# A causal mask added by VectorE, value sums in column quarters, and set-up loads on ScalarE's queue, in a two-layer memory transformer

## The chip, the cores and the metric

The kernel runs on one core of one Trainium2 chip. A core has TensorE (PE: matmuls, with its weight loads shown as PEld), VectorE (DVE), ScalarE (ACT), GpSimd (POOL) and SyncE (SP), which work side by side and are held together by semaphores; 16 DMA engines move data. Matmuls write into PSUM, eight banks of 128 partitions by 512 float32; everything else lives in SBUF. The metric is the device time of one execution in microseconds; the kernel before has a median of 1535.17 us over five runs (1532.09 to 1537.07).

## The reference

Two rounds of the same two layers, A and B, on x of 2048 rows by 448 columns, all in bfloat16:

```python
x = x + _A_ref(_layernorm(x), A_mem0, A_Wq, A_Wk, A_Wv, A_Wo, A_seg_len)
x = x + _B_ref(_layernorm(x), B_W_gate, B_W_up, B_W_down)
x = x + _A_ref(_layernorm(x), A_mem0, A_Wq, A_Wk, A_Wv, A_Wo, A_seg_len)
x = x + _B_ref(_layernorm(x), B_W_gate, B_W_up, B_W_down)
```

A is an attention with a memory that is carried from segment to segment (16 heads of 256, memory M = 8 rows, segments of 32 rows, 64 segments):

```python
mask = (idx[:, None] < M) | (idx[:, None] >= idx[None, :])
mem = mem0
for s in range(n_seg):
    h = concatenate([mem, x[:, s*32:(s+1)*32, :]])           # 40 rows
    q, k, v = h @ Wq, h @ Wk, h @ Wv                         # per head
    p = softmax(where(mask, q @ k.T * scale, -1e9))
    o = (p @ v) @ Wo                                         # summed over heads
    mem = o[:, :M, :]
    outs.append(o[:, M:, :])
```

B is a gated feed-forward layer, `(relu(h @ W_gate) * (h @ W_up)) @ W_down`, with 1792 hidden columns. The rows of one segment depend on those before it only through `mem`, eight rows, so the 64 segments of a round form a chain.

## The kernel before, in words

**What is precomputed.** In set-up, the products M = Wq Wk^T (for the scores) and N = Wv Wo (for the values) are made per head (`products`). Wq, Wk and Wv come in by transposing DMAs of 1024 columns each (`wT`), Wo by plain DMAs (`wo`), each into one of eight slots of the tile `big`. Later the same memory holds U (value sums of both layers), UR (the rider's sums, below) and the feed-forward weights Wg, Wu, Wgu3 and Wd, so those loads wait until the slots are done with.

**The steps.** 68 steps t run one segment of the first round (layer 0) beside one of the second round (layer 1), which lags by four segments. Partitions or columns 0 to 63 mostly hold layer 0, 64 to 127 layer 1. One step, in `step`:

- `h_nat`: the segment's 40 rows per layer, hT, transposed by a DMA into hK.
- `t_units`: hT times M, in five units of row-tiled matmuls (tH) and two full ones (tF) each; copies to TTm (memory queries) and TTs (segment queries) by ACT or DVE (tEm, tEs).
- `s_mem`, the memory rows' scores and softmax (smem, smx), `p_t_mem` (ptm: transposed by TensorE into PTm), `u_mem` (umem: hK times PTm, copied to UTm), `un_mem` (unm: UTm times N, 112 matmuls in four column quarters). ACT copies half the result (XH, L1007), DVE adds the rest (X, L1010, two operations), and `m_t` (mt: five matmuls with the 0/1 matrix selm) puts the new memory into the next step's hT (mtE). This is the chain from step to step.
- `s_seg`, the segment rows' scores (sseg) and softmax (ssx, L860 to L870): maximum, subtraction, exponential (ACT), sum, reciprocal, product into Ps. A DMA transposes Ps into PTs. `u_seg` (useg0 to 3) multiplies hK by PTs, and copies (usE) go to U or UR.
- In every second step: `un`, U times N, for two segments; the layer norm `ln_b`; the feed-forward layer `glu` (glH row-tiled, glF full) and its down product (dn); `out`.

**Riders.** For odd pairs of segments 3 to 29, layer 1's value sums are not made by a matmul of their own: 16 rows of them at a time are copied from UR into free columns of UTm (`ride`, on POOL) and go through unm along with the memory. In those pairs `un` has only layer 0's 64 rows (unc), and so has every pair at the start and end; unc and its down product dnc (first and last pairs only) run as two column halves of the array.

**The causal mask** is a bf16 tile maskr with 0 or -1.6e10. In sseg, the first matmul multiplies it by the identity, which starts the accumulation in PSUM, and the scores are added to it by the matmuls that follow.

**The order.** The program doesn't run its operations as they are written. `_Order` collects them with estimated costs, and a list scheduler fixes the order on each engine at build time, from estimated start times, priorities (BIAS by kind of operation, PERIOD, MODEPEN for a change of tiling mode), SLACK, and RESERVE (PSUM banks kept free). A matmul group has a mode: FULL, ROWS (two 64-row tiles), COLS2, COLS4; a change is charged with SWITCH. `_Sched` then adds semaphore waits. On each engine instructions are issued in the fixed order; one that waits holds all behind it. All DMAs are issued by SP, in one queue.

**Lines.** All matmuls have line L134. L642 and L643 are the copies by ACT and by DVE or POOL; L704 wT, L707 wo, L760 to L766 the feed-forward loads, L806 the transpose of xnA, L926 that of Ps, L940 that of hT; L865, L866, L867, L868, L869 and L870 the softmax; L799 the normalisation in both layer norms.

Of the kernel before, what the change touches and what calls it, by code (L numbers as in the profile page):

```python
# [9 lines left out]
ALU = mybir.AluOpType  # L10
AX = mybir.AxisListType

D = 448
# [153 lines left out]
class _Op:  # L167
    __slots__ = ("i", "kind", "eng", "cost", "fn", "rd", "wr", "name", "mode", "preds", "succs", "prio", "np", "fin", "alloc", "tiles", "ready",
                 "fixed", "bq", "start", "base")


class _Order:
# [11 lines left out]
    def add(self, kind, eng, cost, fn, rd, wr, name=None, mode=0, base=None):  # L184
        o = _Op()
        o.i = len(self.ops)
        o.kind, o.eng, o.cost, o.fn, o.rd, o.wr, o.name, o.mode = kind, eng, cost, fn, list(rd), list(wr), name, mode
        o.succs, o.np, o.alloc, o.ready, o.fixed, o.base = [], 0, [], None, None, base
        self.ops.append(o)
        return o  # L190
# [41 lines left out]
    def ready_at(self, o, e):  # L232
        by = {}
        for q in o.preds:
            if q.fixed == e == "pe":
                continue
            k = q.name if q.fixed == "sp" else q.fixed
            if by.get(k, 0.0) < q.fin:
                by[k] = q.fin
# [8 lines left out]
    def run(self):  # L248
# [40 lines left out]
        while len(order) < total:  # L289
            best = None  # L290
            for e in self.ENGS:
# [7 lines left out]
                if e == "pe":  # L299
                    lst = [(t, o, t + (self.SWITCH if o.mode != mode else 0.0)) for t, o in lst]  # L300
# [4 lines left out]
                for t, o, x in lst:  # L305
                    if x <= lim:
                        p = o.prio
                        if e == "pe" and o.mode != mode:
# [21 lines left out]
            if e == "pe" and o.mode != mode:  # L330
                dur += self.SWITCH
                occ += self.SWITCH
                mode = o.mode
# [24 lines left out]
    def emit(self):  # L358
# [3 lines left out]
        for o in self.order:  # L362
            if o.fixed == "pe":
                self.sc.pe(o.fn(), res(o.rd), res(o.wr), o.fin)
            elif o.fixed == "sp":
                self.sc.dma(o.name, o.fn, res(o.rd), res(o.wr), o.fin)
# [4 lines left out]
BIAS = {"dn.1": -104633.0, "dn.3": -214049.0, "dn.9": -140910.0, "dnE": -786.0, "dnc.11": -139309.0, "dnc.3": 13831.0, "dnc.5": -27812.0,  # L371
    "dnc.7": -6924.0, "glE": -27693.0, "glF0.1": 10010.0, "glF0.11": -174653.0, "glF0.3": -145944.0, "glF0.5": -92812.0, "glF0.7":
    -177072.0, "glF0.9": 19897.0, "glF1.1": -143065.0, "glF1.11": -138570.0, "glF1.3": -105265.0, "glF1.5": -5540.0, "glF1.7": -174301.0,
    "glF1.9": -29011.0, "glF2.1": -153282.0, "glF2.11": -52540.0, "glF2.3": -138423.0, "glF2.5": -124385.0, "glF2.7": -1692.0, "glF2.9":
    -137772.0, "glF3.1": 5447.0, "glF3.3": -104010.0, "glF3.5": 54496.0, "glF3.7": -100124.0, "glF3.9": -120145.0, "glH0.1": 9143.0,
    "glH0.11": -23267.0, "glH0.5": 8524.0, "glH0.7": -139206.0, "glH0.9": 50271.0, "glH1.1": 546.0, "glH1.11": 6320.0, "glH1.3": -616.0,
    "glH1.5": 2773.0, "glH1.7": -2514.0, "glH1.9": 6624.0, "glH2.1": -2112.0, "glH2.11": 2748.0, "glH2.3": -130475.0, "glH2.5": 7362.0,
    "glH2.7": -149344.0, "glH2.9": -112454.0, "glH3.1": -48434.0, "glH3.11": -22235.0, "glH3.3": -113185.0, "glH3.5": 2935.0, "glH3.7":
    3071.0, "glH3.9": -98605.0, "hk": -31963.0, "init": 10044.0, "lna": -13048.0, "lnaC": -8463.0, "lnaT": 25587.0, "lnb": -18913.0, "lnbT":
    -8397.0, "lnbT.11": -8604.0, "lnbTE": 11209.0, "mem": 67030.0, "mt": 400.0, "mt.0": 831.0, "mt.1": -109166.0, "mt.10": -250.0, "mt.2":  # L380
    -28509.0, "mt.3": 7483.0, "mt.5": -625.0, "mt.6": -4647.0, "mt.7": -202.0, "mt.8": -21362.0, "mt.9": -48020.0, "mtE": 11874.0, "prodE":
    11527.0, "prodM.4": 1944.0, "prodN.4": 60.0, "ptm.0": -28767.0, "ptm.1": -55591.0, "ptm.10": -24031.0, "ptm.2": -28108.0, "ptm.3":
    508.0, "ptm.4": 3242.0, "ptm.5": 727.0, "ptm.6": -3533.0, "ptm.7": 929.0, "ptm.8": -1615.0, "ptm.9": -180.0, "ptmE": 1366.0, "pts":
    -38980.0, "pts.11": -20130.0, "ptsE": 1167.0, "ride": 2087.0, "rt": 511.0, "rtT": 13707.0, "smem.0": 20701.0, "smem.1": -2955.0,
    "smem.10": 20594.0, "smem.2": 4096.0, "smem.3": -4245.0, "smem.4": 3195.0, "smem.5": 2453.0, "smem.6": 1626.0, "smem.7": -130185.0,
    "smem.8": -140597.0, "smem.9": 2798.0, "smx": 36317.0, "sseg.1": -387.0, "sseg.10": -79467.0, "sseg.11": 11143.0, "sseg.2": 952.0,
    "sseg.3": 6076.0, "sseg.4": -71071.0, "sseg.5": 282.0, "sseg.6": 279.0, "sseg.7": -132491.0, "sseg.8": -52625.0, "sseg.9": 8111.0,
    "ssx": 5698.0, "tEm": -1049.0, "tEs": -133776.0, "tF0.0": 2987.0, "tF0.1": -445.0, "tF0.10": 4587.0, "tF0.11": 5600.0, "tF0.2": -4684.0,
    "tF0.3": -118385.0, "tF0.4": -349.0, "tF0.5": 3028.0, "tF0.6": -8779.0, "tF0.8": 5120.0, "tF0.9": 51.0, "tF1.1": 5328.0, "tF1.10":
    -11710.0, "tF1.11": -88005.0, "tF1.2": -29557.0, "tF1.3": -6535.0, "tF1.4": 143.0, "tF1.5": 881.0, "tF1.7": -121537.0, "tF1.8":  # L390
    -120291.0, "tF1.9": 850.0, "tF2.0": -27387.0, "tF2.1": -2633.0, "tF2.10": 9137.0, "tF2.11": -433.0, "tF2.2": 14432.0, "tF2.3": -876.0,
# [857 lines left out]
```

## Time and profile before

| | |
|---|---|
| median of five runs | 1535.17 us |
| the profiled execution, in all | 1536.47 us |
| its span, first to last instruction | 1534.7 us |
| mean granted clock of TensorE | 0.994 |
| mask matmuls: 60 of 256 columns, 8 of 128 | 16.4 us busy for the 60, ends modelled |
| unc matmuls, 64 weight columns x 448 | 1008, mean 354 ns |
| unm matmuls, 32 weight columns x 224 | 7504, mean 262 ns |
| rider copies on POOL | 56, mean 961 ns |
| Wo loads, 896 KB, issue to landing | 4, median 6.1 us |
| Wq, Wk and Wv transposes, issue to landing | 4 each, medians 5.9, 5.9, 8.2 us |
| gate and up loads of 448 KB, down loads of 784 KB, to landing | medians 4.6, 6.9 and 7.6 us |

The span is cut into windows, into groups of like instructions, and into a chain of waits that is followed back from the end. Matmuls are pipelined: several are in flight at once, their ends are modelled, and a mean duration is longer than the distance between two starts. So costs of matmuls are read from start to start in the timeline. The idle time before an instruction carries the name of the event that ended it. The granted clock is 1.00 nearly everywhere, 0.50 from about 84 to 97 us and from about 166 to 169 us.

### The profile page before, as it was taken

Reading aid. Unit: us, or ns where it says so; the run is one execution under the profiler, and the core shown is the slowest. Engines: PE = TensorE matmul, PEld = TensorE weight load, DVE = VectorE, ACT = ScalarE, POOL = GpSimd, SP = SyncE. Lnnn points to the kernel's source line nnn. Section 1 sums busy time; section 2 is a strip of 40 time slices with the busy share of each in tenths; the row PEclk is TensorE's granted clock in tenths of the full one; section 3 lists DMA queues with packets and bytes.
Section 4 is the critical chain, followed back from the end, with each engine's and each line's share of the span. In section 5 each row is a group of like instructions: output and inputs, shape, how many; then the busy total and the mean of one; then the engine's idle time right before and its main releaser. Section 6 shows DMA issues by size and latency. Waiting matters only on the chain.

```text
span 1534.7 us, 72243 instructions
## 1 busy us (share of the span) xinstructions
PE 1471.2 (96%) x33360; PEld 1157.7 (75%) x33360; DVE 720.9 (47%) x1911; ACT 797.6 (52%) x2363; POOL 92.4 (6%) x142
## 2 busy tenths in 40 slices
PE   4989998999999999999999999999999999999998
PEld 2568777787878777887877778787877788787776
DVE  4425354543545455344545454354545534453444
ACT  5734555554555546555555555555554555545453
POOL 1000000000000000000000000000000000000000
PEclk9989999999999999999999999999999999999999
DMA  9941111121111111111111111111111111111110
GB/s 216 222 113 33 23 30 24 25 27 25 33 25 29 25 32 28 20 29 29 28 24 34 24 25 27 25 33 24 30 24 33 25 23 30 28 27 25 27 28 18
DMA packets 186462, 59.50 MB, mean 39 GB/s; under 512 B 175256, under 2 KB 185264, under 8 KB 186160
## 3 DMA queue, kind: packets, MB, share of 16 engines
q1 hardware_dynamic: 186160, 54.88, 18.4%
q8 instruction: 262, 4.29, 1.1%
q14 instruction: 40, 0.33, 0.1%
HBM read 10.33 MB, written 1.84 MB: 8 GB/s over the span
## 4 chain that ended last, share of the span: by engine, by line
PE 83%; DVE 6%; DMA 5%; ACT 2%; SPq 2%; issue 1%; POOL 0%
PE P L134 83%; DMA PTs<-Ps 2%; DMA xBT<-xnB 2%; SPq L704 2%; DVE big L643 1%; ACT big L642 1%; DVE xnA L799 1%; DVE X L1010 1%; DVE stat L868 1%; DMA big<-in_A_Wq_dram 1%; DVE stat L865 0%; ACT XH L1007 0%; DMA big<-in_A_Wo_dram 0%; DVE XA L1170 0%; DVE stat L792 0%
## 5 line engine op out<-in xcount | busy, mean ns | idle before, releaser
L134 PE MATMUL P<-hT,Mw 128*128 128x80 bf16 (+1 forms) x11424 | 421.9, 200 | 0.3 <-ACT Mw L642 0.2
L134 PEld LDWEIGHTS P<-hT,Mw 128*128 128x128 bf16 x11424 | 403.0, 100 | 9.2 <-ACT Mw L642 0.3
L134 PE MATMUL P<-Nw,big 128*64 128x448 bf16 (+1 forms) x1904 | 283.9, 353 | 1.4
L642 ACT ACTIVATE TTm<-P 128x96 bf16<-128x96 f32 (+2 forms) x593 | 143.7, 242 | 248.5 <-PE P L134 242.4
L642 ACT ACTIVATE TTs<-P 128x384 bf16<-128x384 f32 (+2 forms) x582 | 263.2, 453 | 0.4 <-DVE TTm L643 0.2
L134 PEld LDWEIGHTS P<-Nw,big 128*64 128x64 bf16 (+1 forms) x1904 | 136.2, 104 | 108.7 <-issue 3.1
L134 PE MATMUL P<-xBT,big 128*128 128x128 bf16 (+3 forms) x3808 | 212.3, 216 | 2.8 <-DMA xBT<-xnB 2.8
L134 PEld LDWEIGHTS P<-xBT,big 128*128 128x128 bf16 (+1 forms) x3808 | 181.0, 97 | 25.0 <-issue 11.1
L134 PE MATMUL P<-Nw,UTm 128*32 128x224 bf16 x7504 | 195.9, 262 | 2.8 <-ACT UTm L642 2.8
L134 PEld LDWEIGHTS P<-Nw,UTm 128*32 128x32 bf16 x7504 | 177.7, 98 | 21.2 <-issue 11.5
L642 ACT ACTIVATE big<-P 128x512 bf16<-128x512 f32 (+1 forms) x346 | 169.5, 548 | 20.9 <-PE P L134 19.9
L643 DVE CAST TTm<-P 128x64 bf16<-128x64 f32 (+3 forms) x87 | 19.8, 228 | 280.4 <-PE P L134 280.2
L643 POOL COPY UTm<-big 128x896 bf16<-128x896 bf16 x56 | 53.8, 961 | 1104.1 <-PE P L134 1104.1
L643 DVE CAST big<-P 128x512 bf16<-128x512 f32 (+1 forms) x166 | 98.6, 619 | 23.7 <-PE P L134 21.8
L1010 DVE TENSOR_TENSOR X<-P,XH 32x224 bf16<-32x224 f32 x134 | 51.1, 381 | 122.0 <-ACT XH L1007 119.4
L134 PE MATMUL P<-PTs,hK 64*128 64x512 bf16 (+1 forms) x640 | 86.6, 339 | 21.0 <-DMA PTs<-Ps 12.4
L865 DVE TENSOR_REDUCE stat<-P 128x8 f32<-128x320 f32 (+3 forms) x135 | 46.1, 351 | 117.0 <-PE P L134 116.7
L134 PE MATMUL P<-big,hB 128*128 128x448 bf16 (+1 forms) x476 | 98.7, 353 | 0.0
L1007 ACT ACTIVATE XH<-P 64x224 f32<-64x224 f32 x67 | 23.6, 352 | 140.5 <-PE P L134 140.2
L134 PE MATMUL P<-hT,M 64*128 64x80 bf16 (+1 forms) x3808 | 92.0, 196 | 3.9 <-issue 1.7
L1140 ACT ACTIVATE gT<-P 128x512 bf16<-128x512 f32 (+2 forms) x136 | 70.7, 522 | 47.7 <-PE P L134 43.7
L134 PEld LDWEIGHTS P<-hT,M 64*128 64x128 bf16 x3808 | 74.6, 96 | 26.0 <-issue 13.4
(91 smaller groups left out, 1217.7 us busy)
## 6 DMA issues: line engine op xcount, KB each, us to landing
big<-in_A_Wo_dram SPq DMA_DIRECT2D x4, 896.0 KB, 6.1
XA<-in_A_x_dram SPq DMA_DIRECT2D x32, 56.0 KB, 2.4
out_dram<-ys SPq DMA_DIRECT2D x32, 56.0 KB, 1.9
big<-in_B_W_down_dram SPq DMA_DIRECT2D x2, 784.0 KB, 7.6
big<-in_B_W_gate_dram SPq DMA_DIRECT2D x3, 448.0 KB, 4.6
big<-in_B_W_up_dram SPq DMA_DIRECT2D x3, 448.0 KB, 6.9
hK<-hT SPq DMA_TRANSPOSE x68, 2.6
PTs<-Ps SPq DMA_TRANSPOSE x67, 2.5
```

The source lines that it names most:

```text
L134: ins = E.matmul(out, lhsT=lhsT, rhs=rhs, **kw)
L642: return E.activation(out(), src(), ACT.Copy)
L643: return E.tensor_copy(out(), src())
L704: S.dma(f"{n}{q}", f"w{k}", lambda E: E.dma_start_transpose(S.slot[k], W[:, q * 1024:(q + 1) * 1024]), (), [("slot", k)], 3950.0, 6300.0)
L799: S.dve(kind, lambda E, a=a, b=b, src=src: E.tensor_scalar(dst[rows, a:b], src, st[rows, so + 6:so + 7], st[rows, so + 8:so + 9], op0=ALU. ...
L865: S.dve(kind, lambda E: E.tensor_reduce(st[:, so:so + n], src(), AX.X, ALU.max), w, rd, [(pre, 0)])
L868: S.dve(kind, lambda E: E.tensor_reduce(st[:, so + 8:so + 8 + n], tmpF, AX.X, ALU.add), w, [kF], [(pre, 1)])
L1007: S.act("xE", lambda E: E.activation(S.XH[64:128, :], T.b()[64:128, 0:224], ACT.Copy), 224, T.res(BOTQ), [("XH",)])
L1010: S.dve("xE", lambda E, r=r, r2=r2, c=c: E.tensor_tensor(S.X[r, c], T.b()[r, 0:224], S.XH[r2, :], ALU.add), 224, T.res((j,)) + [("XH",)], ...
L1140: S.act("glE", lambda E, G=G, k=k, w=w: E.activation(S.gT[:, k % 2, 0:w * n], G.b()[:, 0:w * n], ACT.Relu), w * n, G.res(), [("gT", k % 2)])
```

## The change

It has five visible parts, and a new set of scheduling constants.

1. **Mask.** maskr grows to all 40 keys (zero for the memory's), sseg loses its first matmul, and DVE adds maskr to the scores out of PSUM into Es; the maximum and the subtraction then read Es.
2. **Column quarters.** unc and dnc write 32 rows per matmul in four column quarters (COLS4) instead of 64 in two halves: twice the instructions, half the weight columns in each. mt can run with 64 rows (ROWS) if that is the mode at its place, as only rows 0 to 63 of selm are not zero.
3. **Set-up loads.** The four Wo loads and the ten feed-forward loads are issued by ACT. Each feed-forward load waits for the one two before it. The last Wv transpose is cut into two halves, and the products' operands are tracked by half slots.
4. **Rider copy** on DVE; it is also placed behind the step's X, by a read of ("X", 1).
5. **Scheduler.** New costs for the set-up DMAs, `alt` modes, and new values in BIAS, RESERVE, SLACK and MODEPEN, so that the whole order on every engine is another.

```diff
-        lst = [(t, o, t + (self.SWITCH if o.mode != mode else 0.0)) for t, o in lst]
+        lst = [(t, o, t + (self.SWITCH if mode not in (o.mode, o.alt) else 0.0)) for t, o in lst]
...
-SLACK = {"pe": 101.0, "act": 142.0, "dve": 226.0, "pool": 0.0, "sp": 124.0}
+SLACK = {"pe": 100.0, "act": 91.0, "dve": 324.0, "pool": 500.0, "sp": 0.0}
 PERIOD = 90000.0
-MODEPEN = 42065.0
+MODEPEN = 71087.0
...
-        self.maskr = self.sb("maskr", [128, 8, 32])
+        self.maskr = self.sb("maskr", [128, 8, KEYS])
...
-        def wT(k, n, W, q):
-            S.dma(f"{n}{q}", f"w{k}", lambda E: E.dma_start_transpose(S.slot[k], W[:, q * 1024:(q + 1) * 1024]), (), [("slot", k)], 3950.0, 6300.0)
+        def wT(k, n, W, q, parts=1):
+            w = 8 // parts
+            for j in range(parts):
+                c = q * 1024 + 128 * w * j
+                S.dma(f"{n}{q}" + "ab"[j] * (parts > 1), f"w{k}" + "ab"[j] * (parts > 1),
+                      lambda E, j=j, c=c: E.dma_start_transpose(S.slot[k][:, w * j:w * j + w, :], W[:, c:c + 128 * w]),
+                      (), [("slot", k, j)] if parts > 1 else [("slot", k, 0), ("slot", k, 1)], rate / parts, rate / parts + 2400.0)
...
-            S.dma(f"wo{q}", f"w{k}", lambda E: E.dma_start(S.slot[k], S.Wo_d[:, q * 8:q * 8 + 8, :]), (), [("slot", k)], 2450.0, 4800.0)
+            S.dma(f"wo{q}", f"w{k}", lambda E: E.dma_start(S.slot[k], S.Wo_d[:, q * 8:q * 8 + 8, :]), (), [("slot", k, 0), ("slot", k, 1)], 500.0, 6500.0, "act")
...
-            wT(2 * q, "wv", S.Wv_d, q)
+            wT(2 * q, "wv", S.Wv_d, q, 2 if q == 3 else 1)
...
+        for i, (name, reg, dst, src, key) in enumerate(loads):
+            S.dma("wg", name, lambda E, dst=dst, src=src: E.dma_start(dst, src), S.big_keys(reg) + ([loads[i - 2][4]] if i >= 2 else []), [key], 500.0, 3600.0, "act")
...
-            out = [MM(T.b()[:, 0:8 * KEYS].rearrange("p (a l x) -> p a l x", a=4, l=2)[:, :, l0:l1, 0:SEG], S.ident[:, :],
-                      S.maskr[:, :, :].rearrange("p (a l) x -> p a l x", l=2)[:, :, l0:l1, :], start=True)]
+            out = []
...
-        S.softmax("ssx", src, T.res(), 4 * nl, "ss", v(S.Es[:, :, :]), v(S.Sm[:, :, :]), ("Es",), ("Sm",), dst, ("Ps",), 56, None)
+        S.dve("ssx", lambda E: E.tensor_tensor(v(S.Es[:, :, :]), src(), v(S.maskr[:, :, :]), ALU.add), 4 * nl * KEYS,
+              T.res() + [("mask", j) for j in range(5)], [("Es",)])
+        S.softmax("ssx", lambda: v(S.Es[:, :, :]), [("Es",)], 4 * nl, "ss", v(S.Es[:, :, :]), v(S.Sm[:, :, :]), ("Es",), ("Sm",), dst, ("Ps",), 56, None)
...
-            S.cp("ride", lambda: S.UTm[:, :, 16:32], lambda: S.UR[:, :, 16 * g:16 * g + 16], 16 * NO, [("UR", g // 2, c) for c in range(4)],
-                 [("UTmr",)], eng=("pool",))
+            S.cp("ride", lambda: S.UTm[:, :, 16:32], lambda: S.UR[:, :, 16 * g:16 * g + 16], 16 * NO, [("UR", g // 2, c) for c in range(4)] + [("X", 1)],
+                 [("UTmr",)], speed=3.9, eng=("dve",))
...
+        def mms(mode):
+            r = slice(0, 64 if mode == ROWS else 128)
+            return [MM(T.b()[:, 32 * i:32 * i + 32], S.X[r, c:c + 128], S.selm[r, :], start=True, stop=True) for i, c in enumerate((0, 128, 256, 384, 320))]
+
+        S.mm("mt", mms, 5 * 25.0, [("X", 0), ("X", 1)] + [("sel", j) for j in range(3)], T.res(), alt=ROWS)
...
-                S.mm(f"unc{c_of(k)}", lambda k=k: [MM(T.b()[64 * w:64 * w + 64, 0:D], S.U[:, o + w, cols], S.N[:, o + w, :], start=(o == 0), stop=(o == NO - 2))
-                                         for o in (k, k + 2) for w in range(2)],
-                     2 * S.pitch(D), [("U", l0, s, c_of(k)) for s in range(2)] + nk, T.res(), mode=COLS2)
+                S.mm(f"unc{c_of(k)}", lambda k=k: [MM(T.b()[32 * j:32 * j + 32, 0:D], S.U[:, o + j // 2, 64 * l0 + 32 * (j % 2):64 * l0 + 32 * (j % 2) + 32],
+                                                      S.N[:, o + j // 2, :], start=(o == 0), stop=(o == NO - 2))
+                                                   for o in (k, k + 2) for j in range(4)],
+                     2 * S.pitch(D), [("U", l0, s, c_of(k)) for s in range(2)] + nk, T.res(), mode=COLS4)
...
-                S.mm("dnc", lambda k=k: [MM(T.b()[64 * w:64 * w + 64, 0:D], S.hB[:, 2 * k + w, 0:64], S.Wd[:, 2 * k + w, :], start=(k == 0), stop=(k == 6))
-                                         for w in range(2)], S.pitch(D), [("hB", k // 2)] + wd, T.res(), mode=COLS2)
+                S.mm("dnc", lambda k=k: [MM(T.b()[32 * j:32 * j + 32, 0:D], S.hB[:, 2 * k + j // 2, 32 * (j % 2):32 * (j % 2) + 32], S.Wd[:, 2 * k + j // 2, :],
+                                            start=(k == 0), stop=(k == 6)) for j in range(4)], S.pitch(D), [("hB", k // 2)] + wd, T.res(), mode=COLS4)
```

## The prediction

> **What bounds the kernel now.** I read the page's busy times first: TensorE is busy for 1471.2 of 1534.7 us, VectorE and ScalarE for about half.
>
> ```profile
> PE 1471.2 (96%) x33360; PEld 1157.7 (75%) x33360; DVE 720.9 (47%) x1911; ACT 797.6 (52%) x2363; POOL 92.4 (6%) x142
> ...
> PE 83%; DVE 6%; DMA 5%; ACT 2%; SPq 2%; issue 1%; POOL 0%
> ```
>
> So two things can change the time: matmul time itself, and the 63.5 us in which TensorE stands still. Windows say where these lie: 27.3 us in the first 100 us, 4.5 us after 1500 us, 31.6 us between, some 1.4 us in each round of four steps (87.7 us: the same place of the order stands at 434.45 and at 873.54, five rounds on). The waits between 100 and 1480 us name the causes, largest first (columns: total us, times, longest):
>
> ```profile
> PE P L134 <- DMA PTs<-Ps: 11.8, 12, 1.8
> PE P L134 <- DVE X L1010: 5.7, 7, 1.3
> ```
>
> Third, the timeline of TensorE in one steady step (start, us; starts are exact, ends are modelled, so I go from start to start):
>
> ```profile
> 863.40 0.28 PE L134 MATMUL P<-maskr,ident 128*128 128x256 bf16 x1
> 863.52 0.91 PE L134 MATMUL P<-hT,TTs 128*128 128x40 bf16 x28
> ...
> 877.36 3.61 PE L134 MATMUL P<-hT,Mw 128*128 128x80 bf16 x96
> 880.90 0.60 PE L134 MATMUL P<-hT,M 64*128 64x80 bf16 x24
> 881.44 2.75 PE L134 MATMUL P<-hT,Mw 128*128 128x80 bf16 x72
> 884.03 0.92 PE L134 MATMUL P<-Nw,big 128*128 128x448 bf16 x4
> ```
>
> The mask matmul holds TensorE for 0.12 us. A change of tiling mode has a price too: 96 full-array matmuls take 3.54 us until the row-tiled group starts, 72 take 2.59 to 2.69 us (here, and at 858.66), so 24 cost about 0.86 us and one 0.0358 us; 96 of them are 3.44 us, and 0.10 us is left over for the switch.
>
> Last, set-up: the chain of waits in order of time (start, us, what), and two windows (length and PE busy, the other engines, granted clock, DMA share, GB/s).
>
> ```profile
> 61.56 5.70 DMA big<-in_A_Wo_dram
> ...
> 67.31 9.35 PE P L134 x153
> ...
> 76.68 0.36 ACT XH L1007
> ...
> 81.01 1.67 issue
> ...
> 86.95 1.28 issue
> ...
> 97.91 0.36 ACT XH L1007
> ```
>
> ```profile
> 85.00:90.00 5.00, 3.43 (x60) 2.45 (x57) 1.76 (x9) 1.74 (x9) 0.00 (x0) 0.50 0.93 320
> 90.00:95.00 5.00, 4.00 (x64) 2.61 (x66) 1.47 (x5) 2.05 (x5) 0.00 (x0) 0.50 0.15 34
> ```
>
> TensorE waits for the last Wo load until 67.3, finishes the last products, and then one step (from XH to XH) takes 21.2 us, half of it at clock 0.50.
>
> **Mask on VectorE.** 68 mask matmuls go: 60 of 256 columns at 0.11 us (most pairs of starts show 0.11) and 8 of half the columns at 0.06: **-7.1 us**, certain as long as TensorE sets the pace. VectorE gets 68 additions like the subtraction of L866 (0.485 us for 128x320 out of PSUM, 0.320 for 128x160): 32 us on an engine idle for over half the span. They lengthen the chain scores, softmax, Ps, PTs transpose, useg by 0.49 us. What covers it, step by step: in the new order three steps of four put 8 us or more of other matmuls between sseg and the first useg that needs PTs. The fourth (dn, ptm, dn, umem, dn, unm, useg) has seven dn blocks at 0.378, ptm and umem 0.3, unm 2.70, five switches: 6.2 us, against 7.7 us from the end of sseg at 425.2 to useg at 432.87, of which 1.23 us is seen as idle. Worked through with the rows there, the addition falls partly into the wait for the exponential of the memory softmax, Ps comes 0.4 us later, UTm's copies stand behind the Sm exponential and hold unm for 0.7 us, PTs then for 0.4 us: 1.1 us of idle in the place of 1.25. Queued behind the addition are the last three operations of the memory softmax; ptm behind them has 1.5 us of dn in front of it. I take **0** for the steady part. Bounds: none exposed, or all 67 steps (+32). In the last step the products in front of pts last 2.6 us against a chain of some 3.4: **+0.5**.
>
> **Column quarters.** unc is 28 rounds of two 64-column matmuls: 56 in 5.42 us (831.42 to 836.84), or 0.190 per round without the switch. After, four quarters run in a round. unm shows quarters with 224 columns: 112 in 2.80 us, 0.096 per round; 224 columns more at 1/2.4 ns each make 0.190. So **0** for the work, at most +0.1 us for each of 22 chains (18 unc, 4 dnc). What changes is the mode: unc, dnc and unm now share one, and mt may run row-tiled (32 of 67 do). Counted in the order that each kernel issues, mode changes fall from 760 to 722: 38 x 0.10 = **-3.8 us**. 14 of them lie in the first four steps, where I count time by the chain, so -2.4 remain.
>
> **Set-up.** SP's transposes of Wq and Wk take 3.4 to 4.2 us each, Wv's 3.7 to 8.0, and the windows from 20 to 55 us show DMA shares of 1.06 to 1.17: the engines are full. So moving four Wo loads (0.6 to 0.8 us of issue each) brings little by itself: the same bytes land. I put the last landing at 65.5 instead of 67.26 (bounds 61.5, if the share of 1.40 seen at 55 to 60 holds throughout, and 69, as Wo is now issued behind ScalarE's copies of M, some 8 us later). What helps more is that the last landing is half a Wv block: 7 instead of 14 product groups (0.378 each) remain after it, -2.65; XH comes about 5 us earlier. Then useg of step 0 stands where TensorE waited 1.2 us for XH and X. The ten feed-forward loads leave SP and go in pairs, each behind the load two before it, so fewer transfers crowd TensorE's instruction stream (the two "issue" pieces, 2.95 us, at 320 GB/s). At full clock I add up 13.8 us for the step that took 21.2: hT 0.25, products 5.2, copies 0.7, smem 0.3, softmax 1.9, ptm to UTm 1.4, unm 2.7, XH, X and mt 1.35. Against that, ScalarE now waits in its own queue for loads: five pairs of 896 KB at 4 to 5.5 us put the last issue 16 to 22 us behind the first, and UTm, Sm and XH are queued behind it. First issue about 68.5, so the second XH is at 85.4 at best, about 90 with these stalls and a stretch at half clock: **-8 us** against 97.91. Bounds -13 (no stall, full clock) and +3 (loads as slow as the 7.6 us of the down projection, 4 x 7.6 = 30 us from 68.5, and a window at half clock on top).
>
> The Trainium skill ("Trainium Kernel Development and Optimization", Key Constraints) says that DMAs issued from SP, ACT and POOL share the same 16 engines, and that another issuing engine saves only issue time. By that rule the move would give the four Wo issues, 2.5 us, and the sum would be 1524. The saturated shares agree for Wo; the feed-forward loads also change their pace, which the rule doesn't speak of.
>
> The same skill ("TensorE: Matmul & The Clock Gate", Why this matters for your kernels) asks for idle gaps of over some 3 us before the clock halves. Here it fell to 0.50 at 84 us after pieces of 1.9, 1.1 and 1.7 us. By the rule the new order, with shorter pieces, stays at full clock (sum 1513); by the row it may halve again, which my -8 includes.
>
> **Rider copy.** POOL took 0.96 us, right after unm. On VectorE I bound it by L799 (bf16 in SBUF, 448 elements 0.395 us, 64 elements 0.295: 0.26 ns an element, so 0.5 us for 896) and by casts from PSUM (1.04 ns an element: 1.1 us). Nearest is the first, same memory and type. It stands behind X and in front of hT; in three of four steps other matmuls fill that place. It also takes something away: at 870.72 two L799 operations needed 1.22 us while POOL copied, and X started 0.8 us after XH. Per round that could be worth 0.8 us where X is late. I take **0** for both (bounds -11 over 14 rounds, +14 if 0.25 us shows in 56 copies).
>
> **Sum.** -7.1 - 2.4 - 8 + 0.5 = -17.0, span 1517.7. The profiled execution took 1536.47 in all, 1.3 above the median, so I take the difference from the median: 1535.2 - 17 = **1518 us**, with 1511 to 1525 as this case's own range.
>
> **Rivals.**
> 1. *Set-up gives nothing*: bandwidth decides, and ScalarE's waits return what the smaller last piece gains. Then -7.1 - 3.8 + 0.5: **1525**. For it: DMA shares above 1. Against it: 9.35 us of products behind the last landing, which must shrink.
> 2. *The idle goes too*: set-up -13, and POOL's disturbance of VectorE with it (-11): 1535 - 7.1 - 2.4 + 0.5 - 13 - 11 = **1502**. For it: the 1.22 us pair. Against it: PTs is late in that place whatever X does.
> 3. *Softmax becomes the bound, slower*: if the addition shows in every step, 67 x 0.485 = 32 us against 17 gained: **1550**. It decides from 35 exposed steps of 67 on. For it: PTs is already the largest wait. Against it: it is late in one step of four; that step alone would cost 8 us and leave 1526.
>
> **Numbers.** 0.2% is 3 us, about what can be told from no change. Forecast 0.58, first rival 0.17, second 0.12, third 0.13 (of which 0.05 within 3 us of before). Faster 0.87, same 0.05, slower 0.08. The range reaches into the second and third cases: 1506 to 1533.
>
> **What would show it.** No maskr row on PE, and sseg following smem without the 0.11 us; 722 changes of mode at 0.10; the first XH near 71.5, the second near 90; a round of 87.1 us; the wait for PTs near 12 us. Wrong if PTs or UTm waits of TensorE pass 30 us, if a round is longer than 87.7, or if the second XH is later than 98.

## The result and the profile after

The changed kernel took **1540.2 us** (median of 22 runs, 1535.8 to 1547.0) against 1535.3 (43 runs of the kernel before beside them): ratio 1.0033, 95% interval 1.0024 to 1.0042. It is slower by a third of a per cent, 5 us, where 17 us less were forecast. The profiled execution took 1542.01 us in all, its span is 1540.1 us (before 1534.7).

The page of the changed kernel (busy us, share of the span, instructions; then bytes by DMA queue):

```profile
PE 1468.5 (95%) x34356; PEld 1149.4 (75%) x34356; DVE 785.1 (51%) x2060; ACT 777.5 (50%) x2339; POOL 38.7 (3%) x86
...
q1 hardware_dynamic: 179184, 46.40, 17.7%
q10 hardware_dynamic: 7008, 8.49, 1.8%
```

TensorE did 2.7 us less, but stood still for 71.6 us instead of 63.5. The second queue, q10, is ScalarE's: the Wo and feed-forward loads. The waits of TensorE over the whole span (us in total, times, longest):

```profile
PE P L134 <- DMA big<-in_A_Wk_dram: 18.2, 1, 18.2
PE P L134 <- DMA PTs<-Ps: 13.8, 17, 1.7
PE P L134 <- ACT UTm L645: 10.1, 16, 0.9
PE P L134 <- DVE X L1022: 5.8, 10, 1.3
PE P L134 <- DVE Pm L882: 3.4, 3, 1.2
PE P L134 <- DMA big<-in_A_Wo_dram: 3.3, 1, 3.3
```

The first is the start of the program (16.7 us before, and 2.9 more for Wq). UTm, 2.8 us before, is now 10.1; PTs went from 12.4 to 13.8; neither is near the 30 us that the prediction named as a sign of being wrong. One place of the round, from start to start:

```profile
690.73 0.42 PE L134 MATMUL P<-hT,TTm 128*128 128x40 bf16 x10
690.99 0.91 PE L134 MATMUL P<-hT,TTs 128*128 128x40 bf16 x28
...
695.63 2.87 PE L134 MATMUL P<-Nw,UTm 128*32 128x224 bf16 x112 [0.59 <-ACT UTm L645]
700.18 1.04 PE L134 MATMUL P<-PTs,hK 64*128 64x512 bf16 x10 [1.68 <-DMA PTs<-Ps]
```

No mask row stands in front of sseg any more. The last row shows a wait for PTs of 1.68 us; four rounds later the same place waits 0.23. This will matter below.

The copy XH (ACT) occurs once a step, so its starts cut both spans into pieces. The XH are counted from 0, so the first is XH 0 and the second XH 1:

| piece | before, us | after, us | difference |
|---|---|---|---|
| start to first XH | 76.68 | 81.44 | +4.8 |
| to second XH | 21.23 | 18.51 | -2.7 |
| XH 1 to 12 | 228.26 | 231.49 | +3.2 |
| XH 12 to 61 | 1071.71 | 1069.81 | -1.9 |
| XH 61 to 66 | 103.65 | 106.35 | +2.7 |
| to the end | 33.14 | 32.52 | -0.6 |

The forecast had -8 in the first two rows (they give +2.0) and -9 in the others (they give +3.4). An undisturbed round of four steps is 18.03 + 23.00 + 22.85 + 23.01 = 86.89 us, before 17.64 + 22.00 + 24.89 + 22.96 = 87.50: this -0.61 was forecast, as 87.1 against 87.7. But XH 12 to 61 are 49 steps, 12.25 rounds. At these undisturbed lengths they would have made -6.9 (the odd step is one that grew, from 17.64 to 18.03), and only -1.9 is there: steps above their undisturbed length add 9.1 us after and 4.1 before.

### The profile page after: what moved, and what is told of

It reads as the page before. It is cut to its first block, busy times and chain, and to the rows that moved or that the text cites. A ratio compares the mean times of both kernels' runs of the same rounds, so it can differ in the third digit from the quotient of the medians.

```text
span 1540.1 us, 74134 instructions
## 1 busy us (share of the span) xinstructions
PE 1468.5 (95%) x34356; PEld 1149.4 (75%) x34356; DVE 785.1 (51%) x2060; ACT 777.5 (50%) x2339; POOL 38.7 (3%) x86
## 4 chain that ended last, share of the span: by engine, by line
PE 82%; DMA 7%; DVE 5%; ACT 3%; issue 1%; SPq 1%; ACTq 0%
PE P L134 82%; DMA PTs<-Ps 4%; DMA xBT<-xnB 2%; ACT Mw L645 1%; DMA big<-in_A_Wo_dram 1%; SPq L712 1%; DVE X L1022 1%; DMA big<-in_B_W_up_dram 1%; ACT XH L1019 1%; DVE stat L880 1%; DVE Es L878 1%; DVE big L646 0%; DVE stat L877 0%; ACT UTm L645 0%; DMA big<-in_A_Wk_dram 0%
## 5 line engine op out<-in xcount | busy, mean ns | idle before, releaser
L134 PE MATMUL P<-Nw,big 128*32 128x448 bf16 (+1 forms) x2912 | 288.9, 356 | 1.3 <-DVE big L646 1.1
L645 ACT ACTIVATE TTm<-P 128x96 bf16<-128x96 f32 (+2 forms) x622 | 150.1, 241 | 246.3 <-PE P L134 239.8
L645 ACT ACTIVATE TTs<-P 128x384 bf16<-128x384 f32 (+3 forms) x599 | 270.4, 452 | 0.1
L134 PEld LDWEIGHTS P<-Nw,big 128*32 128x32 bf16 (+1 forms) x2912 | 132.4, 98 | 112.5 <-issue 9.6
L134 PE MATMUL P<-Nw,UTm 128*32 128x224 bf16 x7504 | 198.4, 264 | 10.1 <-ACT UTm L645 10.1
L645 ACT ACTIVATE big<-P 128x512 bf16<-128x512 f32 (+1 forms) x339 | 163.2, 540 | 25.9 <-PE P L134 23.4
L646 DVE CAST big<-P 128x512 bf16<-128x512 f32 (+1 forms) x173 | 104.6, 627 | 111.5 <-PE P L134 109.4
L134 PE MATMUL P<-PTs,hK 64*128 64x512 bf16 (+1 forms) x640 | 82.4, 337 | 17.6 <-DMA PTs<-Ps 13.8
L877 DVE TENSOR_REDUCE stat<-P 128x2 f32<-128x80 f32 (+1 forms) x67 | 15.7, 234 | 158.9 <-PE P L134 158.9
L646 DVE CAST TTm<-P 128x64 bf16<-128x64 f32 (+3 forms) x58 | 12.9, 223 | 163.3 <-PE P L134 163.1
L1157 DVE TENSOR_TENSOR hB<-gT,P 128x512 bf16<-128x512 bf16 (+2 forms) x136 | 78.4, 587 | 14.4 <-ACT gT L1156 8.1
```

The lines of the kernel that those rows point to most:

```text
L134: ins = E.matmul(out, lhsT=lhsT, rhs=rhs, **kw)
L645: return E.activation(out(), src(), ACT.Copy)
L646: return E.tensor_copy(out(), src())
L877: S.dve(kind, lambda E: E.tensor_reduce(st[:, so:so + n], src(), AX.X, ALU.max), w, rd, [(pre, 0)])
L1157: S.dve("glE", lambda E, V=V, k=k, w=w, a=a: E.tensor_tensor(S.hB[:, a:a + w, 0:n], S.gT[:, k % 2, 0:w * n].rearrange("p (i x) -> p i x", ...
```

## The experiments

All kernels keep the order of one of the two kernels (b_: before, a_: after), instruction by instruction, except for what the diff shows; so they tell the edit from the order around it. Each was timed in five rounds beside the kernel before; all ratios are to that kernel, with 95% intervals. The medians come from four sessions in which the kernel before stood at 1534.9 to 1537.7 us, so go by the ratio. For an a_ row the difference from 1.0033 is what its edit does to the changed kernel.

| kernel | order, edit | median, us | ratio |
|---|---|---|---|
| b_mask | before; mask on VectorE | 1559.8 | 1.0166 (1.0142 to 1.0190) |
| b_quart | before; column quarters | 1536.1 | 1.0004 (0.9993 to 1.0015) |
| b_ride | before; rider copy on VectorE | 1534.6 | 0.9990 (0.9982 to 0.9999) |
| b_all | before; these three | 1554.5 | 1.0120 (1.0105 to 1.0135) |
| b_load | before; feed-forward loads on ACT in pairs | 1539.8 | 1.0016 (1.0005 to 1.0027) |
| b_best | before; b_load and b_ride | 1538.1 | 1.0005 (0.9994 to 1.0016) |
| a_wo_act | after; two Wo loads later | 1539.9 | 1.0029 (1.0016 to 1.0042) |
| a_wo_spo | after; Wo issued by SP | 1539.3 | 1.0026 (1.0013 to 1.0039) |
| a_wo_sp | after; both | 1533.9 | 0.9991 (0.9981 to 1.0001) |
| a_ld_sp | a_wo_sp, feed-forward loads on SP too | 1535.3 | 0.9996 (0.9985 to 1.0006) |
| a_mask_pe | after; mask on TensorE again | 1550.9 | 1.0098 (1.0084 to 1.0112) |
| a_add2 | after; mask added twice | 1561.5 | 1.0172 (1.0159 to 1.0186) |
| a_half | after; 64-row halves again | 1543.3 | 1.0057 (1.0039 to 1.0074) |
| a_ride_pool | after; rider copy on POOL again | 1543.6 | 1.0047 (1.0029 to 1.0064) |
| a_order | after; mask, halves, rider, Wo as before | 1552.7 | 1.0111 (1.0095 to 1.0126) |

### One part alone, in the old order

```diff
-                self.sc.op(o.fixed, (lambda E, o=o: o.fn(E, o.fixed)), res(o.rd), res(o.wr), o.fin)
+                if o.pre:
+                    self.sc.op(o.fixed, o.pre[0], res(o.pre[1]), res(o.pre[2]), o.fin)
+                self.sc.op(o.fixed, (lambda E, o=o: o.fn(E, o.fixed)), res(o.rd if o.erd is None else o.erd), res(o.wr), o.fin)
...
-            out = [MM(..., S.ident[:, :], S.maskr..., start=True)]
+            out = []
```

This is b_mask: `pre` is the addition, issued right before the maximum. b_quart takes over the two new matmul lists of unc and dnc, b_ride sets `o.fixed = "dve"` for the rider copy, b_all does the three.

> The order before, on every engine, with the mask alone moved: sseg without its mask matmul, the addition on VectorE right ahead of the maximum. Theory (the matmul time comes off one for one; what the change lost was lost by its new order): the addition is covered in three steps of four, and in the fourth TensorE already waits 0.84 us for X behind PTs; an undisturbed round falls from 87.50 by 0.44 to about 87.06 us, the whole by 7 us to about 1528. Rival (the addition on the softmax chain returns what the matmul gave): a round of 87.5 or more, no gain or a loss, 1535 to 1541.

> The order before with unc and dnc in column quarters alone. Theory: the work takes the same time, 8 changes of mode (between halves and quarters) disappear, -0.8 us, so 1534.5, not to be told from before; a round of 87.40 to 87.50 us. Rival (twice the weight loads and matmuls cost something, or array quarters run 448 columns slower): unc longer than 5.5 us from start to start, up to +0.1 us for each of 22 chains, 1536 to 1538.

> The order before with the rider copy alone moved from POOL to VectorE, at the place that it has in the order, right behind unm and ahead of X. Theory (POOL's copy disturbed VectorE's normalisation and with it X): the copy takes 0.4 us, in which XH is made on ScalarE, X starts within 0.1 us of the end of XH in the fourth step, where it started 0.8 us late, and the round is 0.4 to 0.8 us shorter: 1525 to 1530. Rival (PTs ends that wait anyway, or the copy delays X): a round of 87.5 or more, 1535 or slower.

> The order before with the mask on VectorE, the quarters and the rider copy on VectorE together; loads, half transposes and scheduling constants as before. Theory (the parts are good, the loss sits in the new order and the set-up): -7 for the mask, -0.8 for the modes, -4 to -8 for the rider, less 3 where PTs then ends the wait: about 1523, a round of about 86.6 us. Rival (the parts themselves cost): as slow as the changed kernel or slower, 1535 to 1540.

b_quart is no change. b_ride is worth 1 to 2 us; an undisturbed round falls from 87.50 to 87.26 us, less than the 0.4 to 0.8 of its theory. These are the two zeros of the prediction. b_mask lost 25 us, more than either theory said. (b_all lost 18: with the mask on VectorE, the two other edits gain 7 that they don't gain alone. Why was not followed up.) VectorE's rows of b_mask in one step (start, us):

```profile
1077.21 0.48 DVE L929 TENSOR_TENSOR Es<-P,maskr 128x320 f32<-128x320 f32 x1
1077.72 0.49 DVE L871 TENSOR_REDUCE stat<-Es 128x8 f32<-128x320 f32 x1
...
1080.04 0.49 DVE L876 TENSOR_TENSOR Ps<-Sm,stat 128x320 bf16<-128x320 f32 x1
```

and TensorE's waits over its span:

```profile
PE P L134 <- DMA PTs<-Ps: 19.7, 17, 1.8
...
PE P L134 <- ACT UTm L645: 6.1, 16, 1.1
PE P L134 <- DVE Pm L876: 6.0, 18, 1.2
```

From the end of sseg to the end of the Ps operation it takes 3.30 to 3.63 us in the steps of the round before and 3.70 to 4.09 in b_mask, 0.40 to 0.64 more; and every step of the round became longer, although each lost 0.11 us of matmul: 17.79 + 22.13 + 25.19 + 23.18 = 88.29 us against 87.50. With the 0.44 us of mask matmuls that makes 1.23 us of 1.94 us exposed. The old order had no room for the addition. These longer rounds are some 13 of the 25 us (0.79 in 16.75 rounds); the rest lies in disturbed steps and outside the steady part, and was not taken apart.

### The mask in the new order

a_mask_pe drops the addition and gives sseg its mask matmul back; a_add2 adds maskr to Es a second time.

> The changed kernel with its order frozen, the mask put back on TensorE (68 matmuls of 0.11 us) and the 68 additions on VectorE gone; the score tile in PSUM is read by the maximum and the subtraction again. If the addition is covered in the new order, as the prediction had it: TensorE's 7.1 us come back, 1547. If it is exposed as in the old order (b_mask lost 24 us by the same swap): the waits for PTs and UTm go with it, 1540 - 24 = 1516. If partly: between, and the difference from 1547 is what the addition costs here.

> The changed kernel with its order frozen and the mask addition done a second time on VectorE, 0.49 us more in each step's softmax chain (the output is the same, since the masked scores are so low that their weight is zero either way). If the new order has room: under +3 us, 1540 to 1543, waits of TensorE for PTs and UTm as they are (24 us). If the addition already used up the room: up to 67 x 0.49 = 33 us more, 1573, with the waits for PTs, Pm and UTm doubled.

Here the mask on VectorE is a gain: undoing it costs 0.0065, 10 us, of which 7 are the matmuls by the prediction's price. (In the profile the undisturbed round is 87.72 against 86.89 us; one step grew by 0.60, 0.49 more than its matmul.) But the order leaves no room either: a second addition costs 0.0139, 21 us, 0.32 us a step. In a_add2 the waits for Pm and PTm tell that VectorE's queue holds the memory softmax up (PTm was 1.1 us in the changed kernel):

```profile
PE P L134 <- DVE Pm L885: 7.8, 17, 1.7
...
PE P L134 <- DVE PTm L649: 4.5, 17, 0.5
```

### The set-up loads

```diff
+        for late, mark in (("wo1", "wv1"), ("wo2", "wv2")):
+            a = next(o for o in self.order if o.kind == late)
+            self.order.remove(a)
+            self.order.insert(next(i for i, o in enumerate(self.order) if o.kind == mark), a)
         for o in self.order:
+            if o.kind[:2] in ('wo',):
+                o.fixed = "sp"
```

The first part alone is a_wo_act, the second alone a_wo_spo, both are a_wo_sp.

> The changed kernel with its order frozen, and only two set-up loads moved: the second and third Wo loads are issued later (before the second and third Wv load), so that the fourth, whose products come second in TensorE's order, is the second Wo load on ScalarE's queue. Theory A (order of the Wo loads: TensorE waited for the one that was issued last and was needed second): TensorE no longer stands until 55.8 us, the first XH comes at 77 instead of 81.4, time 1540.2 - 4 = 1536. Theory B (ScalarE's queue: each Wo load took 12 us there against 6 on SyncE's, and held ScalarE's copies): first XH within 1 us of 81.4, time 1539 to 1542.

> The same two loads moved as in a_wo_act, and all four Wo loads issued by SyncE at the places that they hold in the planned order. Theory A (order): the same as a_wo_act, 1535 to 1537. Theory B (ScalarE's queue): Wo lands in 6 us again, ScalarE's copies are not held, first XH at 75 to 77, 1534 to 1536 while a_wo_act stays at 1540. Rival (the DMA engines are full whoever issues): neither of the two is under 1539.

> The changed kernel with its four Wo loads issued by SyncE, at the places that they hold in the planned order, nothing else moved (a_wo_sp also moved two of them). If ScalarE's queue is the whole cost and the order of the loads nothing: 1534, first XH at 75 to 76, second at 93. If the order matters once the queue does not: 1536 to 1538, first XH at 77 to 79.

Neither edit alone did anything that its interval shows; both together gave 0.0042, 6.4 us. The first two XH are at 81.4 and 100.0 us in the changed kernel, 79.7 and 99.6 in a_wo_act, 83.3 and 101.2 in a_wo_spo, and 75.3 and 92.7 in a_wo_sp. The queues and TensorE in the timelines show why. The changed kernel:

```profile
35.41 25.75 SPq L712 DMA_TRANSPOSE big<-in_A_Wv_dram  x4
36.05 1.14 ACTq L716 DMA_DIRECT2D big<-in_A_Wo_dram  x2
37.30 3.44 ACTq L716 DMA_DIRECT2D big<-in_A_Wo_dram  x1
...
42.80 1.23 ACTq L716 DMA_DIRECT2D big<-in_A_Wo_dram  x1
...
55.79 4.02 PE L134 MATMUL P<-big 128*128 128x448 bf16 x12 [3.26 <-DMA big<-in_A_Wo_dram]
```

a_wo_act:

```profile
35.32 24.45 SPq L716 DMA_TRANSPOSE big<-in_A_Wv_dram  x4
...
42.24 0.38 ACTq L720 DMA_DIRECT2D big<-in_A_Wo_dram  x1
...
54.24 3.82 PE L134 MATMUL P<-big 128*128 128x448 bf16 x12 [3.83 <-DMA big<-in_A_Wo_dram]
```

a_wo_spo:

```profile
39.90 6.28 SPq L718 DMA_DIRECT2D big<-in_A_Wo_dram  x4
...
56.50 4.64 PE L134 MATMUL P<-big 128*128 128x448 bf16 x12 [6.40 <-issue]
```

a_wo_sp:

```profile
39.32 3.04 SPq L722 DMA_DIRECT2D big<-in_A_Wo_dram  x2
42.40 4.51 SPq L718 DMA_TRANSPOSE big<-in_A_Wv_dram  x1
46.96 0.58 SPq L722 DMA_DIRECT2D big<-in_A_Wo_dram  x1
...
50.67 2.56 PE L134 MATMUL P<-big 128*128 128x448 bf16 x12 [0.53 <-issue]
57.67 2.44 PE L134 MATMUL P<-big 128*128 128x448 bf16 x12 [0.24 <-DMA big<-in_A_Wv_dram]
```

On ScalarE's queue the Wo loads run beside four Wv transposes that SP issues without a gap, and a Wo load takes 12.0 us (median; 10.0 in a_wo_act). Put on SP all at once, four Wo loads take 10.3 us each and push the second Wv transpose back: it is issued at 46.23 and lands at 56.41, and the second group of products starts at 56.50. Only where SP issues them one or two at a time between the Wv transposes does a load land in 5.6 us (6.1 in the kernel before), and the products run as they come. In the changed kernel the second group of products needs the Wo load that was issued last and the second Wv transpose; both land at 55.70, the group starts at 55.79, and 22 us of matmuls, most of them products, lie behind it. (In the four other kernels with these loads unchanged that Wo load lands 2.4 to 5.6 us after that transpose.) The chain of waits of the changed kernel from there on (start, us, what):

```profile
42.80 12.90 DMA big<-in_A_Wo_dram
...
55.79 21.94 PE P L134 x151
...
79.02 4.46 DMA big<-in_B_W_up_dram
...
83.50 4.99 DMA big<-in_B_W_up_dram
...
99.95 0.36 ACT XH L1019
```

The two pieces of W_up are ScalarE in front of feed-forward loads that wait for earlier ones. What this half of the change is worth was asked in two kernels. a_ld_sp moves these loads to SP and takes their waits for one another away; b_load does the opposite to the kernel before:

```diff
+            if o.kind == "wg":
+                self.sc.dma(o.name, o.fn, res(o.rd + (wg[-2].wr if len(wg) > 1 else [])), res(o.wr), o.fin, "act")
+                wg.append(o)
```

> a_wo_sp with the ten feed-forward loads on SyncE as well, without the wait of each for the one two before it. If ScalarE's queue holds UTm, Sm and XH of the second step behind the loads (ScalarE waited 9.5 us for up loads there in the changed kernel): second XH 3 us earlier than the 92.7 of a_wo_sp, 1531. If ten loads at once crowd the DMA engines and TensorE's instruction stream instead, as in the kernel before (two pieces of 'issue', 2.9 us): second XH at 95 to 98, 1536 to 1539.

> The kernel before with its order frozen and only the ten feed-forward loads changed: issued by ScalarE, each behind the landing of the one two before it. Wo stays on SyncE. Theory (the prediction's reason for the second step: fewer loads at once no longer crowd TensorE's instruction stream): the pieces of 'issue' after the first XH go, the second XH comes 3 to 5 us earlier than 97.9, 1531. Rival (ScalarE waits for loads in front of UTm, Sm and XH and gives it all back): second XH within 1 us of 97.9, 1535.

a_ld_sp has its second XH at 97.4 instead of 92.7 us in the profile, as its second theory said, but 2.7 of these 4.7 us are there at the first XH (78.0 against 75.3), and in the times it differs from a_wo_sp by 0.0005, within the intervals. b_load lost 2.5 us: its first two XH came at 80.0 and 100.7 us, and ScalarE's waits between 70 and 100 us say what it held:

```profile
ACT XH L1011 <- DMA big<-in_B_W_gate_dram: 4.7, 1, 4.7
ACT TTm L646 <- DMA big<-in_B_W_up_dram: 2.8, 1, 2.8
ACT Sm L871 <- DMA big<-in_B_W_up_dram: 1.3, 1, 1.3
```

In the old order an XH stood behind such a load. In the new order the two arrangements can't be told apart by their times.

### Quarters, rider and the order itself

a_half puts the old matmul lists of unc and dnc into the new order, a_ride_pool the rider copy on POOL. a_order is both with a_mask_pe, and with Wo as in a_wo_spo.

> The changed kernel with its order frozen and only the column quarters undone: unc and dnc run again as two 64-column halves, so that the neighbours unm, unc and dnc no longer share a tiling mode. The prediction's term, 0.10 us for each change of mode that the quarters saved, up to 38 of them: 1544. If the mode changes are worth nothing at their places, as in the old order (quarters alone gave 1.0004): 1540.

> The changed kernel with its order frozen and the rider copy back on POOL. If X was a floor under the wait for PTs at the place where three steps in four begin (0.64 us there in the kernel before, with POOL copying beside it), X is late again and the step of 23.0 us becomes 23.4 where PTs is early, 25 where PTs lands late as now: 1540 + 0 to 5. If the rider is worth nothing either way: 1540.

> The order of the changed kernel with the work of the kernel before in it: mask by TensorE, value sums in two halves, rider copy on POOL, Wo loads on SyncE (feed-forward loads stay on ScalarE, the last Wv transpose stays cut in two). Theory (the new order, arranged for the additions on VectorE, is by itself slower than the old one): changed kernel with the mask on TensorE 1551, minus the 6 that Wo on SyncE gave, 1545, quarters and rider 0: 1545 against 1535 of before. Rival (the order is neutral and the four edits carry all of the loss): 1535.

> b_load with the rider copy on VectorE as well (alone 0.999). If the two add: 1530, faster than both kernels. If not: 1534.

Undoing the quarters cost 0.0024, undoing the rider 0.0014; with intervals of 0.0018 on these kernels and 0.0009 on the changed one neither is sure. That a_half came out near the 1544 that was expected is no support for the price of mode changes: counted in the traces, undoing the quarters brings back 7 of them (722 to 729), none in the steady rounds, and the undisturbed round stays at 86.89 us. In the steady part the rider made no difference: the place that follows it takes 23.00 us in a_ride_pool too. a_order says most: the new order with nearly all the old work in it is 17 us slower than the old order, 7 more than its theory had. Some 4.5 us of that are set-up (its second XH is at 102.4). So the edits are worth some 12 us in the new order and lose 18 in the old one (b_all). b_best gained nothing: the rider is worth in it what it was worth alone (0.0011), and b_load's loss takes it away.

### Where the steady part lost its gain

The place shown above (unm, then useg, which needs PTs) opens one step in four. For the twelve rounds between XH 12 and 58, the profile gives the landing time of that PTs transpose and the length of the step that needs it. From the fastest landing to the slowest:

| kernel | landing, us | step, us |
|---|---|---|
| before | 2.5, 2.9, 3.1, 3.2, 3.3, 3.3, 3.9, 4.0, 4.0, 4.0, 4.1, 4.2 | 22.0 in eleven, 21.8 in one |
| after | 2.4, 2.4, 2.4, 2.9, 2.9, 3.3 | 23.0 in all six |
| after | 3.5, 3.7, 4.0, 4.3, 4.3, 4.4 | 23.12, 23.36, 23.63, 23.91, 25.60, 23.98 |
| a_wo_sp, the seven late ones | 3.4, 3.5, 3.6, 3.8, 4.1, 4.1, 4.2 | 23.03, 23.08, 23.18, 23.39, 23.69, 23.75, 23.81 |
| a_mask_pe | 2.4 in seven | 23.11 in all seven |
| a_mask_pe | 4.1 in five | 23.52 to 23.55 |

The landing spreads from 2.4 to 4.4 us in both kernels, and about as often. At this place the old order doesn't notice up to 4.2 us. In the new one the step grows by whatever the landing takes beyond 3.38 us; without the addition (a_mask_pe) by what it takes beyond 3.70. In the changed kernel the excess over 23.0 at this place sums to 5.6 us, 1.7 of it with a stretch at half clock (below). That is the largest part of the 9.1 us of excess; the other three steps of the round add 3.5. The kernel before has its 4.1 us of excess in the other steps; in the first of the round it does notice late landings (0.39 us more at 3.92, 0.48 at 4.01). One profile is not the rule: in the six other kernels with this undisturbed round (a_wo_act, a_wo_spo, a_wo_sp, a_ld_sp, a_half, a_ride_pool) the place costs 2.1 to 4.5 us. This place in the kernel before:

```profile
1046.71 0.82 PE L134 MATMUL P<-PTs,hK 64*128 64x512 bf16 x8 [0.61 <-DMA PTs<-Ps]
...
1048.17 0.39 PE L134 MATMUL P<-PTs,hK 64*128 64x512 bf16 x2 [0.64 <-DVE X L1010]
```

There a second wait, for X, follows the first in the same chain, and a later PTs only shortens it. Where PTs lands early, the waits behind it show the room that each order has: 1.32 us in the kernel before, 0.53 and 0.22 in the changed one, and 1.00 in b_ride, whose rider copy on VectorE lets X come earlier:

```profile
346.23 0.39 PE L134 MATMUL P<-PTs,hK 64*128 64x512 bf16 x2 [1.32 <-DVE X L1010]
```

```profile
438.03 0.39 PE L134 MATMUL P<-PTs,hK 64*128 64x256 bf16 x4 [0.53 <-DVE X L1022]
...
438.75 0.55 PE L134 MATMUL P<-Nw,big 128*128 128x448 bf16 x2 [0.22 <-DVE big L646]
```

```profile
872.60 0.39 PE L134 MATMUL P<-PTs,hK 64*128 64x512 bf16 x2 [1.00 <-DVE X L1012]
```

In the changed kernel useg and mt run straight on after a late PTs (700.18 above). That the wait for X is what hid the spread is borne out by b_ride, the old order with X earlier: the step shrinks from 22.00 to 21.69 us and now grows with a landing beyond 3.99 us (21.85 at 4.15, 21.95 at 4.25), where the kernel before still has 22.00 at 4.16. In the new order the rider moves nothing there (a_ride_pool).

What makes a landing late can be read from the records of single DMA packets in the traces. Beside the queues of SP and ScalarE the page of the changed kernel lists two whose packets it calls "instruction" (packets, MB, share of the 16 engines' time):

```profile
q8 instruction: 270, 4.42, 1.2%
q14 instruction: 40, 0.33, 0.1%
```

The 17 profiles have 1105 PTs transposes from the third step on. In 364 no instruction packet was in flight between issue and landing, and all of these landed in 2.42 to 2.48 us. In the other 741 one was, and all 470 landings above 2.6 us are among these. It counts when the packet comes (one q8 packet of 16 KB alone in that time):

| packet starts, us after the issue | transposes | median landing, us |
|---|---|---|
| 2.0 to 0.3 before it | 90 | 2.45 |
| 0.3 to 0.6 | 28 | 3.11 |
| 0.9 to 1.2 | 53 | 3.63 |
| 1.8 to 2.0 | 83 | 4.01 |
| 2.3 to 2.4 | 45 | 2.46 |

So a late landing is one that met an instruction packet, and this goes by the place in the order: in the kernel before, eleven of the twelve landings at this place took 2.9 us or more; in the changed kernel ten of twelve at another place of the round are above 2.6 us, and two steps later one of twelve. No kernel was made to move these packets alone, so this rests on the times.

In one round the wait also cost clock (windows: length, PE, PEld, DVE, ACT and POOL busy, granted clock, DMA share, GB/s):

```profile
875.00:876.50 1.50, 0.00 (x0) 0.00 (x0) 0.76 (x2) 0.32 (x1) 0.00 (x0) 1.00 0.22 52
...
877.80:881.30 3.50, 3.50 (x16) 1.47 (x13) 1.79 (x4) 1.49 (x6) 0.90 (x2) 0.56 0.24 47
...
701.40:704.90 3.50, 3.50 (x37) 1.82 (x36) 1.83 (x4) 1.54 (x6) 0.91 (x2) 1.00 0.24 47
```

After 1.62 us of idle, 16 matmuls filled 3.5 us in which 37 had started two rounds earlier (the last row), where 1.68 us of idle left the clock at 1.00. This is the step of 25.60: its landing accounts for 0.9 of the 2.6 us, and 1.7 came with the clock.

## Why the prediction was wrong, point by point

**Set-up, -8: failed, 10 us.** The step that failed is "moving four Wo loads brings little by itself: the same bytes land". I priced the last landing. What counts is when the operands of the first products land. Between 46 and 60 us the kernel before starts 62 matmuls on the slots of `big`, a_wo_sp 56, a_wo_act 33, a_wo_spo 22, and the changed kernel 24, because two queues shared the engines and the load needed second was issued last. Even the last landing was no earlier: 67.29 against the 65.5 of the sum (67.26 before). With both mended the second XH is at 92.7, near the 90 that was added up, partly by luck: the first XH is 3.8 us later than the 71.5 forecast, and the step behind it 1.1 us shorter. The Trainium skill ("Trainium Kernel Development and Optimization", Key Constraints), which says that another issuing engine saves only issue time, pointed the right way and not far enough: here the loads landed in 12.0 instead of 6.1 us, and one issue alone took 3.44 us and held ScalarE's copies.

**Softmax addition, 0 in the steady part: the place and the mechanism were right, the size was not.** The undisturbed round is 86.89, as forecast, with 1.34 us of idle at the place that the prediction worked through (0.59 for UTm, 0.75 for X and big where PTs lands early; "1.1 us of idle in the place of 1.25"). What failed is that it took one landing for all: 2.4 to 4.4 us is the spread, and 5.6 us came of it in the profile. The mask's move took 0.32 us of the room (3.38 instead of 3.70), some 1.7 us over the six late steps; the rest is the order's.

**The order as neutral: a term that the sum didn't have.** The edits were priced against the rows of the old order. In the pieces between XH 1 and 12 and 61 and 66 the new order lost 5.9 us, where the forecast had part of its -9. The first loss is in every profile: 231.5 us or more in all a_ kernels, 226.5 to 228.3 in those of the old order without the addition. The second is not sure: 102.8 to 107.5 in the a_ kernels, 102.3 to 107.1 in the b_ ones. In the first of them TensorE's waits for Pm (1.20 us, twice) and UTm (0.9, twice) come within 2 us of each other, and the clock halves there, for 6.8 and 3.4 us; before, it halved there once, for 3.4 us. In the second, PTs is waited for 1.6 and 1.4 us, and the clock halves once. Which decisions of the scheduler cause this stays open; a_order shows only that the order with the old work is slow.

**Mask, -7.1: more.** 10 us in the order that was made for it (a_mask_pe), of which the matmuls are 7.1 by the prediction's price; in the old order -7.1 would have become +25.

**Quarters 0, rider 0: held**, within what the runs can tell. **Modes, -2.4:** the count came out (722 in the trace), but no run tests the price of 0.10 us.

**The last step, +0.5: -0.6** in the one profile.

**Rivals.** The first, "ScalarE's waits return what the smaller last piece gains", names half of what happened, but the loss is in front of the first XH. The third put the loss at the right wait, PTs, with a point of decision (35 exposed steps) that isn't needed: a few late landings are enough when only 9 us are to be gained.

No kernel here is clearly better than the kernel before: b_ride's interval ends just below 1 (0.9990, 0.9982 to 0.9999), and the best in the new order, a_wo_sp, is at 0.9991 (0.9981 to 1.0001), with the mask still on VectorE.

## What to carry to other kernels

Loads that feed a running pipeline are worth what their order of landing is worth: before moving them to a second queue, list which product needs which load and when each lands if the two queues share the engines. In a kernel with a planned order, price an edit in the order that it comes with, and the order with the old work as a term of its own; run the edit alone in both. For a wait at a place with little room take the spread of a transfer's landing from all its rows, not one landing or the median, and look which other packets are in flight when it is late.

## What the runs showed of the hardware

- A stretch at half clock is 3.41 us long, or a multiple of that; half of it is lost, 1.7 us, where TensorE has work throughout (an estimate). Counted in pieces of 3.41 us, the changed kernel has nine (at most 15.3 us lost), the kernel before five (8.5). The Trainium skill ("TensorE: Matmul & The Clock Gate", Why this matters for your kernels) asks for idle gaps of over some 3 us; here 1.62 us of idle, with 0.59 us some 3 us before it, were enough in one round and 1.68 us with the same 0.59 in another were not.
- A 128x512 transpose by DMA lands in 2.42 to 2.48 us where it meets no instruction packet (364 of 364) and in up to 4.9 us where it meets one. The transposes of hT show the same: 2.54 to 2.65 us in 468 without such a packet, a median of 3.5 in 637 with one.
- With Wo on ScalarE's queue the end of set-up varies: the first XH is at 79.7 to 81.4 us in five profiled executions and at 88.7 in a sixth (a_ride_pool).
- The copy of 128x896 bf16 takes 399 ns on VectorE (961 on POOL), against the 0.5 us that was estimated.
